# A gated block of long convolution and MLP on one core: first-layer weights in one transfer, the first layer in 256-token halves, full-shape filter matmuls, and early loads without a chain

## The chip, the cores and the metric

The kernel runs on one core of a Trainium2 chip. The metric is the device time of one execution in microseconds (us); lower is better. "The kernel before" and "the kernel after" are the two versions. The span of a profile, from the first to the last instruction, is about 2 us shorter than the device time.

In the profile PE is TensorE's matmuls, PEld its weight loads, DVE is VectorE, ACT is ScalarE, POOL is GpSimd and SP is SyncE, whose queue issues most DMA. A name with a q at the end (ACTq) is the engine's sequencer, which issues its instructions and DMA. PSUM is the memory that TensorE writes its results to; copying them out is called eviction. The "taps" are the weights of the 4-tap shift, brought into place by TensorE and ACT.

## The reference

```python
x = A_q                                            # 2048 tokens x 640, bf16
g = sigmoid((x * gate_w).sum(-1, keepdims=True))
# branch A: 4-tap shift of k, times v, a convolution over all 2048 tokens, times q
kv = shift(k, shift_k) * v
y  = irfft(rfft(pad(kv)) * rfft(pad(ssm_k)))[:2048] + kv * ssm_D
a  = q * y
# branch B: LayerNorm, first layer, token shifts by +1, -1, +2, -2 of the four quarters, second layer, MLP
h  = gelu(layernorm(x) @ w1)
x1 = x + shift_quarters(h) @ w2
b  = x1 + gelu(layernorm(x1) @ w3) @ w4            # 640 -> 1536 -> 640
out = g * a + (1 - g) * b
```

The kernel does the convolution as a folded discrete Fourier transform with matmuls. "Filter matmuls" transform the filter `ssm_k`, in five chunks of 128 features. "Chunks" of branch B are four groups of 512 tokens; a tile is 128 tokens. `mm1` to `mm4` are its four layers.

## The kernel before

The program is recorded as about 1200 operations with the memory that each reads and writes. A list scheduler then orders them for all engines at once; semaphore waits follow from the order. A table of about 350 numbers ("biases"), found by search, shifts the priorities. So the order of each engine's instructions is fixed at build time.

Large loads are chained: each waits for the landing of an earlier one.

```python
# in schedule()
if o.cost > 500 and not o.tp:                     # a large load that is not a transpose
    gate = [(ops[d].end, d) for d in done if ops[d].end <= st]
    if gate:
        o.preds.setdefault(max(gate)[1], False)   # wait for an earlier DMA
```

The first-layer weights come in eight transfers of small rows on ACT's queue, that is in the queue of the engine that also evicts PSUM:

```python
w1d = B_w1.rearrange("(c p) (g f) -> p c g f", p=128, g=4)
for g in range(4):
    P.dma("act", w1[:, g], w1d[:, :, g, 0:128])                              # rows of 256 B
for g in range(4):
    P.dma("act", w1[:, 4, :, 32 * g:32 * (g + 1)], w1d[:, :, g, 128:160])    # rows of 64 B
```

Each first-layer chunk is done at 512 tokens; its last feature tile is evicted in four 32-row pieces:

```python
def mm1(sc):
    xt = chunk_of[0, sc]
    ...                                            # gate products, 20 matmuls of one column
    for ft in range(5):
        pr = ps(1, "mm1")                          # one PSUM bank
        mm(pr, [(w1[:, ft, c], xt[:, c, :]) for c in range(DC)])
        if ft < 4:
            act(hT[:, ft, 2 + 512 * sc:2 + 512 * (sc + 1)], pr, ACTF.Gelu_apprx_tanh)
        else:
            for g in range(4):
                ...                                # 32 rows each, shifted
```

Two kinds of filter matmuls do not use the full 128 x 128 array:

```python
pairs = [(Rh[...], ev[...]) for kk in range(2)]
if y == 0:
    pairs.append((ones[0:1, :], ev[0:1, 1, :, 0, :]))              # 1 row
mm(pr[:, r, :], pairs, low=[(Zn[:, kk, :], ev[:, 0, :, kk, :])     # 32 columns
                            for kk in range(2)] if j == 0 and r == 1 else [])
```

Tokens of tiles 0 to 3 are transposed by TensorE and evicted by ACT; those of all later tiles by DMA. For `ln2`, ACT squares each tile for its sum alone, and the squared tile is discarded into `xn2[t % 2]`, the buffer from which a transposing DMA later reads:

```python
act(xn2[t % 2], X[:, t, :], ACTF.Square, scale=D ** -0.5, accum=st[1, 1][:, t:t + 1])
```

## Time and profile before

| | before |
|---|---|
| time, median of 4 runs | 261.24 us (260.86 to 263.06) |
| span of the profile | 259.0 us |
| first matmul of the first layer | 19.3 us |
| matmul time needed after the warm-up | 223.3 us |

The last row is my sum over all matmuls of the pitch (time from start to start) that undisturbed stretches of the trace show: 0.136 us for 320 columns, 0.216 us for 512 and 0.025 us for one, which columns / 2.4 ns plus 2.5 ns, and 0.025 us at least, fits.

The profile's page of the kernel before: the span, the busy line of all engines, and the busy tenths of each engine in 40 slices of 6.5 us (PEclk is the granted TensorE clock in tenths; DMA is the busy share of the 16 DMA engines).

```profile
span 259.0 us, 4011 instructions
...
PE 239.6 (93%) x1488; PEld 138.5 (53%) x1488; DVE 221.4 (85%) x337; ACT 166.6 (64%) x306; POOL 59.4 (23%) x93
...
PE   7189799999899999999999989999999999999970
...
DVE  4659378989798984438999899999999999999885
ACT  2172699879889985999934366323832275437993
...
PEclk9855999999999999999999999999999999999996
DMA  6999978996889999997124010000000000003776
...
```

PE is at 9 nearly everywhere except in the first 30 us and the last 8. This does not by itself prove a limit, because ends of matmuls are modelled. The start-to-start pitches do: after 30 us only 8.9 us of PE's time are not filled at full pitch. The page shows DVE at 9 from 150 to 240 us and DMA at mostly 7 to 9 for the first 120 us.

Three pieces of the chain that ended last (start us, length us, what). Buffer numbers are left out of names, so all four weights read `in_B_w_dram`; at this place it is the first layer's:

```profile
...
2.88 8.86 DMA arena<-in_B_w_dram
...
12.18 0.70 ACT arena L997
...
19.16 8.61 PE PSall L1008 x30
...
```

The same place in the timeline (start us, length us, engine, line, operation; in brackets the engine's idle time before it and what ended it):

```profile
...
3.92 8.22 ACTq L229 DMA_DIRECT2D arena<-in_B_w_dram  x4
...
12.18 0.69 ACT L997 ACTIVATE arena<-PSall 4x640 bf16<-4x640 bf16 x1 [8.37 <-DMA arena<-in_B_w_dram]
...
19.16 9.21 PE L1008 MATMUL PSall<-arena 128*128 128x1 bf16 x47 [0.30 <-ACT arena L997]
...
20.12 0.15 PEld L1008 LDWEIGHTS PSall<-arena 128*128 128x128 bf16 x1 [0.28 <-issue]
20.54 0.15 PEld L1008 LDWEIGHTS PSall<-arena 128*128 128x128 bf16 x1 [0.28 <-issue]
...
```

ACT's queue is held for 8.2 us by four of the weight transfers. The eviction at 12.18 us, which needs nothing but the taps, stands behind it. The first-layer matmuls begin within the group at 19.16 us (gate products first). The last two lines are weight loads of that group, 0.42 us apart, so a 512-column matmul takes 0.43 us instead of 0.216: half clock.

Weight loads by shape (count, total busy us, mean ns, then idle before and what ended it):

```profile
...
L1008 PEld LDWEIGHTS PSall<-arena 128*128 128x128 bf16 x1417 | 131.9, 98 | 98.0 <-ACT arena L997 9.5 <-issue 8.0 <-DVE arena L987 2.1
...
L1008 PEld LDWEIGHTS PSall<-arena 1*128 1x128 bf16 x10 | 0.9, 90 | 4.2 <-issue 4.2
L1008 PEld LDWEIGHTS PSall<-arena 128*32 128x32 bf16 x10 | 0.6, 94 | 1.1 <-issue 1.1
...
```

A load of 1 row or of 32 columns is no dearer than a full one (90 to 98 ns), but the ten 1-row loads have 4.2 us of idle time before them, put down to "issue". In the trace, a matmul on either side of a change of shape starts 0.31 us after the one before, not 0.216.

### The profile page before, as it was taken

The numbers are of one execution on the slowest core, as the hardware profiler recorded it, in microseconds if no ns is written. First come the engines' busy times: TensorE is split into PE (matmuls) and PEld (weight loads), VectorE is DVE, ScalarE is ACT, GpSimd is POOL, SyncE is SP. The second block draws the span as 40 slices with busy tenths as digits, with TensorE's granted clock in tenths as the row PEclk, the third lists the DMA queues.
The fourth block names the chain that finished last, engine by engine and source line by source line (L and its number), as shares of the span: only waits on it lengthen the run. The fifth ranks groups of instructions, "written<-read, shape, count | busy, mean of one in ns | idle before, by whom it ended". The sixth has DMA issues, their size and how long they took to land.

```text
span 259.0 us, 4011 instructions
## 1 busy us (share of the span) xinstructions
PE 239.6 (93%) x1488; PEld 138.5 (53%) x1488; DVE 221.4 (85%) x337; ACT 166.6 (64%) x306; POOL 59.4 (23%) x93
## 2 busy tenths in 40 slices
PE   7189799999899999999999989999999999999970
PEld 3063456744645464455466734566447754777750
DVE  4659378989798984438999899999999999999885
ACT  2172699879889985999934366323832275437993
POOL 2220054753970445113075500000000000000000
PEclk9855999999999999999999999999999999999996
DMA  6999978996889999997124010000000000003776
GB/s 174 273 257 179 324 253 137 195 239 179 171 187 237 225 257 240 281 288 221 36 51 124 16 25 9 16 3 0 0 3 0 0 4 0 0 3 110 210 187 202
DMA packets 66567, 34.42 MB, mean 133 GB/s; under 512 B 38008, under 2 KB 64884, under 8 KB 66548
## 3 DMA queue, kind: packets, MB, share of 16 engines
q1 hardware_dynamic: 59692, 32.71, 51.4%
q10 hardware_dynamic: 6712, 0.92, 2.7%
q0 software_dynamic: 144, 0.54, 0.7%
q8 instruction: 11, 0.18, 0.3%
q14 instruction: 8, 0.07, 0.1%
HBM read 24.34 MB, written 2.62 MB: 104 GB/s over the span
## 4 chain that ended last, share of the span: by engine, by line
PE 50%; DVE 21%; DMA 9%; ACT 9%; POOL 6%; issue 3%; ACTq 1%; POOLq 0%; SPq 0%
PE PSall L1008 50%; DVE arena L987 20%; ACT arena L997 9%; DMA arena<-arena 5%; POOL arena L992 4%; DMA arena<-in_B_w_dram 3%; POOL arena L1175 2%; DMA out_dram<-arena 1%; DVE arena L992 1%; ACTq L229 1%; DVE arena L1171 0%; POOLq L1402 0%; ACT L997 0%; DVE arena L1172 0%; SPq L226 0%
## 5 line engine op out<-in xcount | busy, mean ns | idle before, releaser
L1008 PE MATMUL PSall<-arena 128*128 128x320 bf16 (+4 forms) x1445 | 231.7, 319 | 10.3 <-ACT arena L997 9.1
L987 DVE TENSOR_TENSOR arena<-arena 128x640 bf16<-128x640 bf16 (+5 forms) x235 | 194.6, 877 | 9.7 <-ACT arena L997 7.5
L1008 PEld LDWEIGHTS PSall<-arena 128*128 128x128 bf16 (+2 forms) x1445 | 134.4, 98 | 107.5 <-issue 13.4
L997 ACT ACTIVATE arena<-PSall 128x640 bf16<-128x640 f32 (+5 forms) x186 | 118.1, 686 | 42.2 <-PE PSall L1008 33.0
L992 POOL TENSOR_SCALAR arena<-arena 128x1 f32<-128x1 f32 (+2 forms) x60 | 35.3, 592 | 85.7 <-ACT arena L997 64.7
L997 ACT ACTIVATE arena<-arena 128x640 bf16<-128x640 bf16 (+5 forms) x55 | 33.5, 619 | 21.1 <-DVE arena L987 11.5
L997 ACT ACTIVATE arena<-PSall,arena 128x640 bf16<-128x640 f32 (+1 forms) x32 | 20.4, 651 | 23.0 <-PE PSall L1008 22.9
L992 DVE TENSOR_SCALAR arena<-arena 128x640 bf16<-128x640 bf16 (+1 forms) x37 | 14.4, 402 | 18.1 <-POOL arena L1175 15.8
L1175 POOL TENSOR_TENSOR arena<-arena 128x1 f32<-128x1 f32 (+1 forms) x25 | 22.2, 889 | 1.4
L1171 DVE BATCH_NORM_STATS2 arena<-arena 128x6 f32<-128x320 bf16 x32 | 14.2, 477 | 4.8 <-DMA arena<-in_A_q_dram 4.8
L1034 PE MATMUL PSall<-arena 128*128 128x512 bf16 x18 | 5.6, 481 | 1.6 <-DVE arena L1030 1.6
L1034 PEld LDWEIGHTS PSall<-arena 128*128 128x128 bf16 x18 | 2.1, 120 | 4.6 <-issue 1.9
L997 ACT ACTIVATION_READ_ACCUMULATOR arena<-arena 128x1 f32 x16 | 3.4, 210 | 0.0
L997 ACT ACTIVATION_READ_ACCUMULATOR arena<-PSall 128x1 f32 x16 | 3.3, 204 | 0.0
L1172 DVE BATCH_NORM_AGGREGATE arena<-arena 128x2 f32<-128x12 f32 x16 | 2.8, 200 | 0.0
L997 ACT ACT_TABLE_LOAD x1 | 1.3, 1283 | 2.3 <-issue 2.3
L1226 PE MATMUL PSall<-arena 128*128 128x128 bf16 x20 | 2.5, 309 | 0.0
L1067 PE MATMUL PSall<-arena 128*4 128x128 bf16 x5 | 0.4, 218 | 2.1 <-DMA arena<-in_A_shift_k_dram 2.1
L1226 PEld LDWEIGHTS PSall<-arena 128*128 128x128 bf16 x20 | 2.0, 139 | 0.0
L992 DVE TENSOR_SCALAR arena<-PSall 128x4 f32<-128x4 f32 x4 | 0.6, 153 | 1.4 <-PE PSall L1008 1.4
L1067 PEld LDWEIGHTS PSall<-arena 128*4 128x4 bf16 x5 | 0.3, 83 | 2.6 <-DMA arena<-in_A_shift_k_dram 2.6
L987 POOL TENSOR_TENSOR arena<-arena 128x16 f32<-128x16 f32 x3 | 1.4, 476 | 0.5 <-DVE arena L992 0.4
(16 smaller groups left out, 3.4 us busy)
## 6 DMA issues: line engine op xcount, KB each, us to landing
arena<-in_A_k_dram SPq DMA_DIRECT2D x14, 400.0 KB, 4.5
arena<-in_A_q_dram SPq DMA_DIRECT2D x20, 160.0 KB, 2.5
arena<-in_A_v_dram SPq DMA_DIRECT2D x16, 160.0 KB, 4.7
arena<-in_A_ssm_k_dram SPq DMA_DIRECT2D x5, 512.0 KB, 4.5
out_dram<-arena SPq DMA_DIRECT2D x16, 160.0 KB, 2.3
arena<-in_A_q_dram SPq DMA_DIRECT2D x3, 640.0 KB, 5.7
arena<-in_B_w_dram SPq DMA_DIRECT2D x1, 1920.0 KB
arena<-in_B_w_dram SPq DMA_DIRECT2D x1, 1152.0 KB
```

Of the source, the lines that this page charges most:

```text
L229: fn = lambda e: e.dma_start(out, in_, **kw)
L987: P.op(eng, lambda e: e.tensor_tensor(o, a, b, op), [a, b], [o], dve_ns(o, [a, b], 2) if eng == "dve" else 500)
L992: P.op(eng, lambda e: e.tensor_scalar(o, real(a), s1, s2, op0=op0, **({} if op1 is None else {"op1": op1})), [a] + aps, [o], dve_ns(o, [a] ...
L997: P.op("act", lambda e: e.activation(o, real(a), f, bias=bias, scale=scale, **({"accum_out": accum} if accum is not None else {})), [a] + ...
L1008: fns.append(lambda e, part=part, l=l, r=r, i=i: e.matmul(real(o)[0:32] if part else real(o), l, r, start=(i == 0), stop=(i == last)))
L1034: P.op("pe", [lambda e: e.matmul(real(pw), warm[:, 0:128], warm[:, 128:640], start=True, stop=True)] * 2, [warm], [pw], 856.0)
L1067: P.op("pe", [lambda e, c=c: e.transpose(real(psb)[:, 128 * c:128 * (c + 1)], shk_sb[:, 4 * c:4 * c + 4], ident) for c in range(DC)], [shk ...
L1171: P.op("dve", lambda e, o=o, i=i: e.bn_stats(o, i), [i], [o], 400)
L1172: P.op("dve", lambda e: e.bn_aggr(bna[:, t, :], bns[k]), [bns[k]], [bna[:, t, :]], 120)
L1175: P.op("pool", lambda g: g.tensor_tensor(o, a, e, ALU.pow), [a, e], [o], 450 + 400 * n_of(o))
L1226: P.op("pe", [lambda e, c=c, pb=pb, xn=xn: e.transpose(real(pb)[:, 128 * c:128 * (c + 1)], xn[:, 128 * c:128 * (c + 1)], ident) for c in r ...
```

## The change

The intent is to get TensorE to real work sooner and to keep it there. It loads the first-layer weights with 1280 B rows in one transfer on SP, after four x tiles; splits the first layer of chunks 0 and 1 into halves of 256 tokens; transposes tiles 4 to 7 on TensorE too; pads the odd filter matmuls to 128 x 128 with zeros; and leaves early loads out of the chain. The bias table is new as a whole.

```diff
-                if o.cost > 500 and not o.tp:
+                if o.cost > 500 and not o.tp and not o.early:
...
-    w1d = B_w1.rearrange("(c p) (g f) -> p c g f", p=128, g=4)
-    for g in range(4):
-        P.dma("act", w1[:, g], w1d[:, :, g, 0:128])
-    for g in range(4):
-        P.dma("act", w1[:, 4, :, 32 * g:32 * (g + 1)], w1d[:, :, g, 128:160])
+    P.dma(sp, w1, B_w1.rearrange("(c p) f -> p c f", p=128), early=True)
+    act(w1x..., w1...[:, :, :, 128:160], ACTF.Copy)     # collects the last feature tile
...
-                    pairs.append((ones[0:1, :], ev[0:1, 1, :, 0, :]))
-                mm(..., low=[(Zn[:, kk, :], ev[:, 0, :, kk, :]) ...])
+                    pairs.append((Zn[:, 2, :], ev[:, 1, :, 0, :]))
+                if j == 0 and r == 1:
+                    pairs += [(Zn[:, kk, :], ev[:, 0, :, kk, :]) for kk in range(2)]
...
-            if t >= 4:
+            if t >= PET:                                # PET = 8: tiles 4 to 7 turned by TensorE
...
-        at(mm1, sc)
+        for k in (0, 1) if sc < 2 else (None,):         # halves in chunks 0 and 1
+            at(mm1, sc, *(() if k is None else (k,)))
+        at(mmg, sc)                                     # gate products apart
...
-    WARM = 9
+    WARM = 12                                           # 24 warm-up matmuls, not 18
-    BIASES = {...}
+    BIASES = {...}                                      # all values new
```

Cut: the loads of x for later chunks become two per chunk, the table of the filter transform moves from POOL's queue to SP's, the scheduler's engines begin at small offsets instead of 0, tiles 2 and 3 are normalised one by one, two costs in the scheduler's model change, an unused branch of `ln1` goes.

## The prediction

> **What bounds it now.** The page: span 259.0 us, TensorE (PE) busy 93%, DVE 85%, ACT 64%. The windows view shows three stages. From 0 to 30 us PE is badly fed: in the timeline the first-layer matmuls start at 19.2 us and chunk 0 of that layer ends at 28.4 us. From 30 to 251 us PE is back to back: the matmuls there, at their pitch in the trace (0.136 us for 320 columns, 0.216 us for 512), fill all but about 5 us. Then comes a tail of 7.5 us. VectorE is nearly as full (100% from 150 to 240 us), and DMA is near 100% until 120 us.
>
> **Why it starts late.** The chain of waits begins with 8.9 us of first-layer weight DMA: ACT's queue is stuck issuing small-row transfers (one group of issues spans 3.9 to 12.1 us), so the taps' eviction waits until 12.2 us. The same traffic delays the later x tiles (about 8 and 11.5 us) and the taps' input (6.7 us to landing). PE goes idle, and the layer's first 13 or so matmuls run at half clock, 0.43 us instead of 0.216 (clock row: 0.50 from 15 to 25 us), about 3 us lost. The Trainium skill, "TensorE: Matmul & The Clock Gate", section "What's actually happening", says that an idle window throttles the clock to half; this trace agrees.
>
> **What the change does.**
> 1. Weights in one transfer with 1280 B rows, behind four x tiles: ACT's queue is free; x tiles and taps land by 5 to 6 us. About 2.5 MB end with the weights; at the trace's 260 GB/s that is some 10 us plus 2 us to landing. I expect the layer's first matmul at 12 to 13 us, 6 to 7 us earlier, perhaps at full clock.
> 2. Halves, and PE transposes for tokens 4 to 7: PE keeps its columns plus 20 transposes (1.1 us); ACT gains some 6 us, and will pace PE between 12 and 30 us. By 30 us I expect chunks 0 and 1 and one second-layer tile done: 7 us ahead of before.
> 3. Full-shape filter matmuls: around each 1-row and 32-column group the pitch is 0.31 us instead of 0.216; six switches a chunk at 0.1 us, five chunks: 3 us, all on PE's chain.
> 4. Unchained early loads, and four DMA transposes fewer (1.3 us of SP queue each): they let DMA and VectorE keep up with the earlier PE; no separate gain.
> The re-tuned order gives nothing certain; 0 to 2 us may go to new PE waits on VectorE and DMA.
>
> **Prediction.** 7 + 3 us off 261.4: **251.0 us**, range 247.0 to 256.0. Faster by over 2%: 0.89; within 2%: 0.10; slower: 0.01.
>
> **What would show it.** First-layer matmuls from about 12.5 us; no 8 us issue on ACT's queue; x tiles landed by 6 us; pitch 0.216 us around filter matmuls; PE continuous from about 30 us, ending near 241 us; tail still 7 to 8 us; PE busy time 3 to 6 us lower.
>
> **What would make it wrong.** The filter and table loads (1 MB) ahead of the weights make them land after 15 us; the second-layer weights, k or v come late, standing behind 1.3 MB of x; VectorE, full in the last 100 us, does not move forward with PE, so PE waits for the products; or PE still starts at half clock.

## The result, and the profile after

| | before | after |
|---|---|---|
| median of 4 runs each | 261.24 us | 253.15 us |
| range | 260.86 to 263.06 | 252.32 to 253.76 |
| span of the profile | 259.0 us | 250.5 us |
| first matmul of the first layer | 19.3 us | 13.5 us |

The ratio is 0.9675, with a 95% interval of 0.9622 to 0.9728. The kernel is faster by 3.2%, and the time lies inside the predicted range.

The page after, the same rows as before:

```profile
span 250.5 us, 4194 instructions
...
PE 236.6 (94%) x1564; PEld 143.4 (57%) x1564; DVE 223.0 (89%) x337; ACT 171.9 (69%) x327; POOL 73.0 (29%) x94
...
PE   7999999999999999999997979999999999999990
...
DVE  5678889849999998898988899999999999998685
ACT  2699996999788999797724572236622286727993
...
PEclk9999999999999999999999999999999999999998
DMA  6999999987799996596522210000000000303676
...
```

The hole in PE's first 30 us is gone; the rest looks as before, and DVE now fills more of its row.

The pieces of the chain that ended last at the same place:

```profile
...
3.08 6.22 DMA arena<-in_A_ssm_k_dram
9.32 4.09 ACT arena L1012 x7
13.46 6.11 PE PSall L1021 x70
...
```

And the timeline at the same places:

```profile
...
4.12 0.43 SPq L230 DMA_DIRECT2D arena<-in_B_w_dram  x1
...
7.82 0.69 ACT L1012 ACTIVATE arena<-PSall 4x640 bf16<-4x640 bf16 x1 [3.94 <-PE PSall L1077]
...
13.46 6.11 PE L1021 MATMUL PSall<-arena 128*128 128x256 bf16 x70 [0.46 <-ACT arena L1012]
...
```

The weights are issued at 4.1 us in 0.4 us, ACT evicts the taps at 7.8 us, when TensorE has made them, and the first layer starts at 13.5 us instead of 19.3, at full pitch (0.109 us for 256 columns). It waits last for ACT's evictions of transposed tokens, no longer for weights.

The full-shape weight loads after, where the "issue" part of their idle time was 8.0 us and is 0.5 us (part of the 8.0 is the half clock at the start; the other two shapes are gone):

```profile
...
L1021 PEld LDWEIGHTS PSall<-arena 128*128 128x128 bf16 x1487 | 137.8, 98 | 92.4 <-ACT arena L1012 9.6 <-DVE arena L1002 2.8 <-issue 0.5
...
```

Waits, before and then after (waiter, what it waited for, us in total, times, longest):

```profile
...
PE PSall L1008 <- ACT arena L997: 9.1, 7, 3.2
...
ACT arena L997 <- DMA arena<-arena: 7.8, 3, 4.3
...
```

```profile
...
ACT arena L1012 <- DMA arena<-arena: 11.5, 8, 3.0
...
PE PSall L1021 <- ACT arena L1012: 4.6, 7, 1.6
...
```

PE waits less for ACT, but ACT now waits more often for transposing DMAs (`arena<-arena`): that is the new wait, and run 8 below is about it.

The ledger of PE, worked out from the starts of the matmuls in the two profiled traces (us; both hold as many matmuls as weight loads, so no record is missing). "Lost" is pitch beyond the undisturbed one.

| | before | after |
|---|---|---|
| useful matmul time issued by 30 us | 9.2 | 18.4 |
| useful matmul time in all | 223.3 | 224.6 |
| lost after 30 us at changes of shape | 3.0 | 0.0 |
| lost after 30 us in gaps of 0.25 us or more | 4.9 | 6.3 |
| lost after 30 us in smaller ones | 1.0 | 1.3 |
| from the last matmul's end to the span's end | 5.4 | 6.3 |

So 9.2 us of a head start, less 1.2 us of added matmuls; plus 3.0 us of shapes; less 1.7 us of new waits and 0.9 us of tail. That makes 8.3 of the span's 8.5 us (the rest is rounding and the last matmul's own length).

The head start is more than the earlier start of the layer, which is 5.8 us. Between that start and 30 us the kernel before loses about 2.9 us at half clock (14 matmuls, the first and last of them in part) and 1.8 us in a wait at 28.2 us for ACT, which evicts the last feature tile in four 32-row pieces; the kernel after loses 0.8 us. By the layer's start, the kernel after had done 0.5 us less of other matmuls. No run here takes away the half clock of the kernel before alone.

### The profile page after: what moved, and what is told of

The parts are those of the page before. It is cut to its first block, busy times and chain, and to the rows that moved or that the text cites. A ratio compares the mean times of both kernels' runs of the same rounds, so it can differ in the third digit from the quotient of the medians. Undisturbed runs are those within 1.5% of the kernel's fastest.

```text
span 250.5 us, 4194 instructions
## 1 busy us (share of the span) xinstructions
PE 236.6 (94%) x1564; PEld 143.4 (57%) x1564; DVE 223.0 (89%) x337; ACT 171.9 (69%) x327; POOL 73.0 (29%) x94
## 4 chain that ended last, share of the span: by engine, by line
PE 44%; DVE 17%; ACT 14%; DMA 11%; POOL 9%; issue 3%; SPq 1%; DVEq 0%; ACTq 0%; POOLq 0%
PE PSall L1021 43%; DVE arena L1002 15%; ACT arena L1012 14%; DMA arena<-arena 8%; POOL arena L1007 7%; DMA arena<-in_A_ssm_k_dram 2%; POOL arena L1187 2%; DVE arena L1007 1%; DMA arena<-in_A_q_dram 1%; SPq L230 1%; PE PSall L1228 1%; DVEq L443 0%; ACTq L443 0%; DVEq L441 0%; POOLq L441 0%
## 5 line engine op out<-in xcount | busy, mean ns | idle before, releaser
L1021 PE MATMUL PSall<-arena 128*128 128x320 bf16 (+4 forms) x1495 | 225.9, 311 | 5.9 <-ACT arena L1012 4.6
L1021 PEld LDWEIGHTS PSall<-arena 128*128 128x128 bf16 (+1 forms) x1495 | 138.4, 98 | 93.4 <-ACT arena L1012 9.6
L1012 ACT ACTIVATE arena<-PSall 128x640 bf16<-128x640 f32 (+8 forms) x206 | 121.5, 645 | 26.4 <-PE PSall L1021 21.6
L1007 POOL TENSOR_SCALAR arena<-arena 128x1 f32<-128x1 f32 (+2 forms) x61 | 46.2, 761 | 59.2 <-ACT arena L1012 39.7
L1012 ACT ACTIVATE arena<-arena 128x640 bf16<-128x640 bf16 (+4 forms) x55 | 34.5, 629 | 29.6 <-DVE arena L1002 15.8
L1012 ACT ACTIVATE arena<-PSall,arena 128x640 bf16<-128x640 f32 (+1 forms) x32 | 20.4, 660 | 16.8 <-PE PSall L1021 16.7
L1187 POOL TENSOR_TENSOR arena<-arena 128x1 f32<-128x1 f32 (+1 forms) x26 | 25.5, 984 | 1.6
L1183 DVE BATCH_NORM_STATS2 arena<-arena 128x6 f32<-128x320 bf16 x32 | 13.6, 476 | 3.9 <-DMA arena<-in_A_q_dram 3.9
L1047 PE MATMUL PSall<-arena 128*128 128x512 bf16 x24 | 7.9, 492 | 1.6 <-DVE arena L1043 1.6
L1047 PEld LDWEIGHTS PSall<-arena 128*128 128x128 bf16 x24 | 2.7, 121 | 5.7 <-issue 3.2
L1228 PEld LDWEIGHTS PSall<-arena 128*128 128x128 bf16 x40 | 2.3, 97 | 1.0 <-DVE arena L1183 0.4
L1141 DVE MEMSET arena<- 32x480 uint32 x2 | 0.9, 458 | 0.1
```

Source lines behind the costliest of these rows:

```text
L1007: P.op(eng, lambda e: e.tensor_scalar(o, real(a), s1, s2, op0=op0, **({} if op1 is None else {"op1": op1})), [a] + aps, [o], dve_ns(o, [a] ...
L1012: P.op("act", lambda e: e.activation(o, real(a), f, bias=bias, scale=scale, **({"accum_out": accum} if accum is not None else {})), [a] + ...
L1021: fns.append(lambda e, l=l, r=r, i=i: e.matmul(real(o), l, r, start=(i == 0), stop=(i == last)))
L1047: P.op("pe", [lambda e: e.matmul(real(pw), warm[:, 0:128], warm[:, 128:640], start=True, stop=True)] * 2, [warm], [pw], 856.0 if i < 4 els ...
L1141: P.op("dve", lambda e: e.memset(kt[0:32, 0:3, :], 0.0), [], [kt[0:32, 0:3, :]], 500)
L1183: P.op("dve", lambda e, o=o, i=i: e.bn_stats(o, i), [i], [o], 400)
```

## The experiments

My theory is the ledger: the early start and the shapes give the gain, because TensorE has no slack after 30 us. Rivals: the re-tuned table gives it; the clock gives it; VectorE sets the end, so that TensorE's savings come back as waits.

To undo one part alone, the order must not move. In the runs said to have "the same order" the scheduler was given the other build's order and PSUM places, operation by operation; waits are then worked out anew from the memory that is touched. Fed back to the unchanged kernel after, this reproduced it: a build of both programs differs in line numbers only. The helper's lines shift in these files, so line numbers differ from those above. All twelve kernels gave the correct result. Every call had its own runs of the kernel before; their medians were 261.51, 261.65 and 261.62 us.

| run | median us (range of 4) | ratio to before, 95% interval |
|---|---|---|
| 1 after, odd shapes put back | 255.48 (254.31 to 255.86) | 0.9763, 0.9721 to 0.9805 |
| 2 before, full shapes alone | 259.79 (258.75 to 260.47) | 0.9937, 0.9886 to 0.9988 |
| 3 after, small-row weights on ACT's queue | 263.77 (263.67 to 264.48) | 1.0094, 1.0057 to 1.0130 |
| 4 after, small-row weights on SP's queue | 257.13 (256.66 to 258.71) | 0.9845, 0.9799 to 0.9890 |
| 5 after, early loads chained | 253.75 (253.02 to 254.47) | 0.9707, 0.9678 to 0.9737 |
| 6 after, no real warm-up | 253.80 (253.17 to 254.13) | 0.9706, 0.9680 to 0.9732 |
| 7 after, whole 512-token chunks | 261.66 (261.31 to 263.50) | 1.0024, 0.9984 to 1.0065 |
| 8 after, squares into a free buffer | 251.45 (251.04 to 252.45) | 0.9624, 0.9588 to 0.9660 |
| 9 before, empty table | 287.23 (285.00 to 287.32) | 1.0945, 1.0893 to 1.0997 |
| 10 after, empty table | 307.99 (307.29 to 308.54) | 1.1757, 1.1716 to 1.1798 |
| 11 after, whole chunks, their own order | 266.65 (264.95 to 268.09) | 1.0178, 1.0111 to 1.0244 |
| 12 after, tiles 4 to 7 turned by DMA | 257.79 (256.88 to 258.01) | 0.9845, 0.9808 to 0.9881 |

### 1. The odd filter shapes put back into the kernel after

```diff
-                    pairs.append((Zn[:, 2, :], ev[:, 1, :, 0, :]))
-                if j == 0 and r == 1:
-                    pairs += [(Zn[:, kk, :], ev[:, 0, :, kk, :]) for kk in range(2)]
+                    pairs.append((ones[0:1, :], ev[0:1, 1, :, 0, :]))
+                mm(..., low=[(Zn[:, kk, 0:32], ev[:, 0, :, kk, :]) ... if j == 0 and r == 1 else []])
```

> The kernel after, in the same order on every engine, with the ten 1-row and ten 32-column filter matmuls put back in place of the full-shape ones. My theory (a change of shape costs TensorE about 0.1 us each time, six times a chunk, and TensorE has no slack there): 253.2 plus 2.5 to 3.2, so 255.7 to 256.4 us. Rival (the switches hide behind waits for VectorE and DMA, which set the pace): within 1 us of 253.2.

Measured: 255.48 us, 2.3 us more than 253.15 (the two ranges of four do not overlap, though the intervals of the ratios just touch). Weight loads by shape in this run:

```profile
...
L1186 PEld LDWEIGHTS PSall<-arena 1*128 1x128 bf16 x10 | 0.9, 90 | 4.2 <-issue 4.2
...
L1186 PEld LDWEIGHTS PSall<-arena 128*32 128x32 bf16 x10 | 0.6, 94 | 1.1 <-issue 1.1
...
```

The idle time before the two shapes is back to the figure of before, 4.2 and 1.1 us, and the ledger has 3.0 us lost at 30 changes of shape (12 of the 1564 matmul records are missing from this trace). My theory holds, a little below its stated range; the rival, under 1 us, does not.

### 2. Full shapes alone in the kernel before

The edit is that of the change, with the table of zeros widened from 64 to 384 columns.

> The kernel before, in its own order, with full-shape filter matmuls alone. My theory: 261.2 minus 2.5 to 3.2, so 258.0 to 258.7 us. Rival: VectorE, full from 150 us on in the trace of before, sets the end, so TensorE's 3 us come back as waits and the time stays within 1 us of 261.2.

Measured: 259.79 us, 1.7 us less, with an interval of the ratio from 0.9886 to 0.9988. So it helps, but with a little over half of the 3.0 us that PE's ledger loses at these places. In this run's ledger nothing is lost at changes of shape; 13 of the 1488 matmul records are missing from its trace, and allowing for those (2.6 us), the losses after 30 us are 7.1 us where before had 8.9. The 1.8 us between them answer to the time; about 1.2 of the 3.0 us came back as waits, 0.5 us of it in the last gap before the end (2.6 us at 249 us, for 2.1 at 251). Both accounts have a share. The layer began 1.1 us later in this run (20.4 us), yet by 30 us TensorE had done as much as in the kernel before (allowing for one missing record), so a small shift at the start need not reach the end.

### 3 and 4. The weights in eight small-row transfers again

```diff
-    P.dma(sp, w1, w1s, early=True)
+    w1op = P.dma("act", w1, w1s, early=True)            # run 3; sp in run 4
+    w1op.fns = [lambda e, a=a, b=b: e.dma_start(w1[:, :, a:b], w1s[:, :, a:b])
+                for a, b in [(160*g + 128, 160*g + 160) for g in range(4)]
+                          + [(160*g, 160*g + 128) for g in range(4)]]
```

> The kernel after, in the same order, with the first-layer weights again in eight small-row transfers (256 B and 64 B rows) on ACT's queue. My theory (the weight load is what delayed the start): the first layer starts 3 to 6 us later than 13.5 us, ACT's queue is stuck for some us, and the time rises to 256 to 259 us. Rival (the start is set by the tokens, taps and transposes, and the weights have slack): at most 1 us slower.

> The same eight small-row transfers, but issued by SP in the place of the one transfer, so that ACT's queue stays free. If the row size and the traffic are what costs: nearly as slow as with ACT's queue, 255 to 258 us. If the stuck ACT queue is what costs: within 1.5 us of 253.2.

Measured: 263.77 us on ACT's queue, 10.6 us more than the kernel after and 2.3 us more than before; 257.13 us on SP's, 4.0 us more. ACT's timeline in run 3:

```profile
...
4.10 13.06 ACTq L1233 DMA_DIRECT2D arena<-in_B_w_dram  x6
17.21 0.69 ACT L1177 ACTIVATE arena<-PSall 4x640 bf16<-4x640 bf16 x1 [13.30 <-issue]
...
```

ACT's sequencer sits on six issues for 13.1 us, and everything that ACT should evict waits. The first layer starts at 23.5 us, 10.0 us later than in the kernel after, and the time grows by nearly the same 10.6 us: here a later start passes straight through to the end. (The layer's first 12 matmuls run at half clock in this run, 1.2 us of pitch.) TensorE's timeline in run 4:

```profile
...
11.26 1.54 PE L1396 MATMUL PSall<-arena 128*128 128x128 bf16 x20
15.53 4.78 PE L1186 MATMUL PSall<-arena 128*128 128x256 bf16 x27 [2.73 <-DMA arena<-in_B_w_dram]
```

Here ACT is free and TensorE waits 2.7 us for the weights themselves; the layer starts at 15.5 us, and the x loads and second-layer weights behind it come later too: the eight issues hold SP's queue for 8.3 us, and the next x load is issued at 12.5 us instead of 4.6. So about 4 us belong to eight small-row transfers instead of one, the held SP queue included, and another 6.6 us to having them in ACT's queue. Row size and number of transfers were changed together. Nor is row size all: in the kernel after, two of SP's issues of long rows (x and second-layer weights) took 2.0 and 1.8 us, where others took 0.4. What stretches an issue is not shown. My forecast for run 3 (256 to 259) was too low by 5 us, since I had not thought that the same order would put all six issues ahead of ACT's first eviction.

The Trainium skill ("DMA: Bandwidth & Descriptors", section "Issuing engines are not separate DMA queues") says that issuing from several engines saves only the sequencer's time to start a DMA, "which is usually small relative to the DMA itself". In this trace it is not small: 13.1 us of one sequencer for six of the eight transfers, when all the weights in one transfer took 0.43 us to issue in the kernel after.

### 5. The early loads chained again

```diff
-EARLY = lambda o: o.early
+EARLY = lambda o: False       # for the waits only; the order is the same
```

> The kernel after, in the same order, with the early loads chained again: each large load waits for the landing of an earlier one, as in before. My theory: the chain holds back the loads behind the first tokens by some us, so the first layer starts 1 to 4 us later and the time rises by 1 to 4 us, to 254 to 257. Rival (the queue is full anyway, and order alone matters): within 0.7 us of 253.2.

Measured: 253.75 us, 0.6 us more, which the intervals do not separate from nothing. The first layer starts at 13.6 us instead of 13.5. In this order the chain hardly bites; the rival is right. The run says nothing of the chain in the kernel before, where two of its waits stand in ACT's queue.

### 6. No real warm-up

```diff
-e.matmul(real(pw), warm[:, 0:128], warm[:, 128:640], start=True, stop=True)
+e.matmul(real(pw)[:, 0:32], warm[:, 0:128], warm[:, 128:160], start=True, stop=True)
```

> The kernel after, in the same order, with the 24 warm-up matmuls cut from 512 to 32 columns, so that TensorE does nearly nothing before its first real work. If the clock state at the first layer matters: the granted clock is 0.5 for the first 3 to 6 us of the first layer, and the time rises by 1.5 to 3 us, to 254.7 to 256.2. If ACT's evictions pace the first layer (I predicted so): within 1 us of 253.2.

Measured: 253.80 us, 0.65 us more and not separated from nothing. The profile shows the layer beginning at 12.9 us with 9 matmuls of 256 columns at a pitch of 0.213 us, twice the usual 0.109: half clock, but for only 2 us. The start itself is no later than with the warm-up (12.9 to 13.6 us in runs 1, 5 and 8). Half clock costs 1.1 us of pitch here, and 0.65 us or less of it reaches the time. The number meets my second expectation, but not for its reason: the stretch was short, and ACT did not pace the layer. The run prices the warm-up of the kernel after. It does not price the half clock of the kernel before (2.9 us in the ledger), so the clock as a rival is only in part refuted. This is the place to warn of the clock column (a stretch of the windows view: busy us of each engine with its count, then the granted clock, DMA share and GB/s):

```profile
...
core 0: us, PE busy (x) PEld busy (x) DVE busy (x) ACT busy (x) POOL busy (x), PEclk, DMA share, GB/s
13.00:16.00 3.00, 3.00 (x19) 2.24 (x19) 2.80 (x9) 2.59 (x6) 0.71 (x2) 1.00 1.07 362
...
```

The column says 1.00 from 13 to 16 us, where the pitch says half. The Trainium skill ("TensorE: Matmul & The Clock Gate", section "Seeing it yourself") warns that these clock events have been "observed to be unreliable"; this trace agrees. (In the kernel before, the column did show 0.50 from 15 to 25 us, where the pitch is half.) The pitch between matmuls is the better witness.

### 7 and 11. Whole chunks in the place of halves

```diff
-        for k in (0, 1) if sc < 2 else (None,):
+        for k in (None,):
```

> The kernel after, in the same order, with the first layer of chunks 0 and 1 in whole 512-token matmuls in the place of the second half. The first layer must wait for four transposed tokens, not two: about 1.4 us later in the trace of after (13.5 to 14.9 us), while ACT saves about 3 us of evictions. My theory: 253.2 plus 0.5 to 2 us. Rival (ACT paces this stage): 253.2 or less.

Measured: 261.66 us, 8.5 us more: all of the gain. TensorE's timeline from 14 to 40 us:

```profile
...
15.27 7.47 PE L1184 MATMUL PSall<-arena 128*128 128x512 bf16 x45 [1.66 <-ACT arena L1175]
22.60 0.72 PE L1391 MATMUL PSall<-arena 128*128 128x128 bf16 x10
24.74 1.80 PE L1184 MATMUL PSall<-arena 128*128 128x320 bf16 x12 [1.42 <-ACT arena L1175]
26.39 0.72 PE L1391 MATMUL PSall<-arena 128*128 128x128 bf16 x10
28.22 7.20 PE L1184 MATMUL PSall<-arena 128*128 128x512 bf16 x37 [1.11 <-ACT arena L1175]
37.56 2.88 PE L1184 MATMUL PSall<-arena 128*128 128x320 bf16 x14 [2.14 <-ACT arena L1175]
```

The layer starts at 15.3 us (1.8 us later, and the 6 first matmuls are at half clock), and then TensorE waits for ACT before each group: 1.4, 1.1 and 2.1 us. With halves, ACT evicts the first half while TensorE does the second, and the first second-layer tile needs only the first half. With whole chunks, in this order, the two engines take turns; in the kernel before, TensorE's wait for ACT at 28.2 us is of the same kind. I had expected 0.5 to 2 us. The order was made for halves, though, so in run 11 the scheduler ordered whole chunks itself:

> The kernel after with whole 512-token matmuls in chunks 0 and 1, as in the run that took 261.7 us, but here the scheduler makes its own order for them (the table kept, its entries for the halves gone). If the 8.5 us of that run came from an order made for halves: 254 to 256.5 us here. If halves are needed to keep ACT and TensorE overlapped at the start whatever the order: 258 us or more.

Measured: 266.65 us, slower still. This meets the number that I had named for "halves are needed whatever the order" (258 or more), but run 11 lacks tuned entries for its new operations, and runs 9 and 10 show what a missing entry can cost. Two orders out of very many don't prove that no order would do.

### 8. The discarded squares into a free buffer

ACT's line in the kernel after, in the stretch of the longest gaps of TensorE:

```profile
...
129.08 0.74 ACT L1012 ACTIVATE arena<-arena 128x640 bf16<-128x640 bf16 x1 [3.02 <-DMA arena<-arena]
...
132.68 0.74 ACT L1012 ACTIVATE arena<-arena 128x640 bf16<-128x640 bf16 x1 [2.77 <-DMA arena<-arena]
...
133.41 1.46 ACT L1012 ACTIVATE arena<-PSall,arena 128x640 bf16<-128x640 f32 x2
...
```

ACT waits 3.0 and 2.8 us for transposing DMAs that still read the buffer into which the square is discarded; since ACT works in order, the PSUM eviction at 133.41 us, for which TensorE waits, stands behind it.

```diff
-        act(xn2[t % 2], X[:, t, :], ACTF.Square, ...)
+        act(xn2[t % 2] if t < 8 else xn1[2], X[:, t, :], ACTF.Square, ...)   # and placed behind its eviction
```

> The kernel after, with one fix: for tiles 8 to 15 the discarded output of ACT's squares goes to a free buffer instead of the one that the transposes still read, and the squares stand right behind their evictions. My theory: ACT's 11.5 us of waits for transposes, and TensorE's two gaps of 1.8 and 1.6 us at 132 and 144 us that come from ACT standing still, mostly go; 253.2 minus 1.5 to 3 us. Rival: VectorE is full from 150 us, so the gaps only move: within 0.7 us of 253.2.

Measured: 251.45 us, 1.7 us less by medians. The same stretch in this run:

```profile
...
132.09 0.79 ACT L1175 ACTIVATE arena<-PSall,arena 128x640 bf16<-128x640 f32 x1 [7.49 <-PE PSall L1184]
133.86 0.79 ACT L1175 ACTIVATE arena<-PSall,arena 128x640 bf16<-128x640 f32 x1 [0.97 <-PE PSall L1184]
...
```

ACT's waits for transposes are gone, and with them TensorE's gaps at 132 and 144 us (1.8 and 1.6 us). But four squares now stand between ACT's evictions from 102 to 107 us, where the kernel after has two, and a new gap opens there, at 106 us:

```profile
...
PE PSall L1184 <- ACT arena L1175: 1.5, 1, 1.5
```

Gaps of 0.25 us or more after 30 us sum to 5.85 us, where the kernel after has 6.34. So the gaps mostly moved, as the rival said, though the time did improve: this is the fastest kernel of the study. Its interval (0.9588 to 0.9660) overlaps that of the kernel after (0.9622 to 0.9728), so the step over the kernel after is likely but not settled. The run changes two things, the buffer and the place of the squares in ACT's order; which of them counts was not tested.

### 9 and 10. Both kernels with an empty table

```diff
-    P.biases.update(BIASES)
+    P.biases.update({})
```

> The kernel before with its table of order biases emptied: its scheduler orders by its own rule alone. Theory (the change of structure gives most of the 8 us): both kernels lose by the same kind of amount and the kernel after with an empty table stays 5 us or more ahead of this one. Rival (the re-tuned table gives the gain): both without a table end within 3 us of each other.

> The kernel after with its table of order biases emptied. Theory: 5 us or more faster than the kernel before with an empty table. Rival: within 3 us of it. Either way slower than 253, by how much I can't say: 258 to 275.

Measured: before 287.23 us, after 307.99 us. Both of my statements fail: without its table the kernel after is not 5 us ahead, nor is it within 3 us, but 21 us behind, and its time is far outside the 258 to 275 that I named. Its longest wait of TensorE for ACT is 29 us:

```profile
...
PE PSall L1021 <- ACT arena L1012: 41.5, 15, 29.0
...
```

The table is worth 26 us to the kernel before and 55 us to the kernel after, several times the whole change. So the change cannot be split cleanly into structure and order: the gain is that of a structure and an order fitted to it. The runs at a fixed order show what each part does inside that order, and nothing more.

### 12. Tiles 4 to 7 turned by DMA again

```diff
-    PET = 8
+    PET = 4
```

> The kernel after, in the same order, with tokens of tiles 4 to 7 transposed by DMA again (1.2 us of SP queue each, some 3 us to landing) in the place of TensorE and ACT. My prediction gave this part no gain of its own. If that is right: within 1 us of 253.2. If the SP queue and the landing hold back chunk 1: 255 to 259 us, with TensorE waiting for a DMA near 22 us.

Measured: 257.79 us, 4.6 us more. TensorE:

```profile
...
24.42 4.54 PE L1184 MATMUL PSall<-arena 128*128 128x256 bf16 x25 [2.68 <-DMA arena<-arena]
29.94 6.32 PE L1184 MATMUL PSall<-arena 128*128 128x256 bf16 x50 [0.97 <-DMA arena<-arena]
```

It waits 2.7 and 1.0 us for transposing DMAs before the two halves of chunk 1. I had given this part no gain of its own; inside this order it carries 4.6 us.

## Why the prediction was right, and where it was not

The time (253.15 us for 251.0, in a range of 247 to 256) and the sign were right.

- **The head start was right.** "6 to 7 us earlier" for the first layer: 19.3 to 13.5 us, 5.8 us. "7 us ahead of before" by 30 us: 9.2 us of useful matmuls more, 8.0 after taking off the added ones. Run 3 shows that a shift of the start by 10.0 us shifts the end by 10.6 us. The size owes something to luck: the start itself moved less than forecast, and the rest of the 9.2 us came from half clock and a wait for ACT, for which the sum has no term. "ACT's queue is stuck issuing" holds for 6.0 of its 8.2 us; 2.2 us were waits of the chain, which the prediction counted for nothing.
- **The shapes were right in mechanism and too large in time.** "3 us, all on PE's chain": PE's ledger loses exactly 3.0 us there, and none after. But undone in the kernel after it costs 2.3 us and alone in the kernel before it gives 1.7 us: not all of it was on the chain.
- **The size that was missing** is the sentence "0 to 2 us may go to new PE waits". I named it and took nothing off. The ledger has 1.7 us more of waits after 30 us and 0.9 us more of tail. TensorE's last matmul ended at 244 us, not near 241. That is more than the distance to 251; the head start, 1 us larger than forecast, made up for some, so part of the closeness is errors that cancel.
- **"ACT … will pace PE between 12 and 30 us" did not happen.** TensorE lost 0.8 us from the layer's start at 13.5 us to 30 us. Run 7 shows why the halves matter there: in that order they are what keeps ACT from pacing it.
- **"Perhaps at full clock" was right; its worth is open.** In before, half clock costs the layer 2.9 us of pitch, part of the head start above. Run 6 shows only that without its warm-up the kernel after has 1.1 us of half clock and loses 0.65 us, within the noise.
- **"No separate gain" for the unchained loads and the transposes was half right.** Chaining again costs 0.6 us, within the noise; the transposes by DMA cost 4.6 us.
- **"The re-tuned order gives nothing certain" was the weakest sentence.** Order is worth more than everything else here (runs 9 and 10). Undoing single parts inside the tuned order costs 10.6, 8.5, 4.6, 2.3, 0.6 and 0.6 us, in sum over three times the gain; a likely reason, not shown, is that the order was fitted to all of them. What a table newly searched for the old structure would reach is open; no run here can say.

## What to carry to other kernels

Where TensorE is back to back to the end, look at when it starts: a much later start can pass through to the end nearly in full (run 3), and the cause may be a compute engine whose own queue is stuck issuing small-row DMA. Put such issues on a queue that evicts nothing, in as few transfers as possible, and cut the first work so that the evicting engine can begin while TensorE goes on. In a statically ordered kernel, undo a part with the order held before saying what it is worth, and do not add such costs up.

## What the Trainium skill lacked or had wrong

- "TensorE: Matmul & The Clock Gate" (section "Step-by-step: what each phase is for") says that weight loads are pulled ahead of running matmuls where row groups don't conflict or the load goes to the background buffer. Neither it nor "TensorEngine Tiling (Array Packing)", which has a change of tiling mode drain TensorE, gives a price for a change of array shape: here each change to or from a 1-row or 32-column matmul costs about 0.1 us (pitch 0.31 instead of 0.216 us for 512 columns), although the loads themselves take 90 to 98 ns in any shape. Whether these changes are such a drain is not shown.
- "DMA: Bandwidth & Descriptors" calls the sequencer's time to start a DMA usually small. "Perfetto Trace Analysis" does describe a sequencer as taken up until a DMA's descriptors are made. What both lack is how long that can be for an engine with other work: six transfers of 256 B and 64 B rows held ACT for 13.1 us (run 3).
- "TensorE: Matmul & The Clock Gate" is right that clock events are unreliable. For a cross-check it names a throttle counter; the pitch serves too: 0.213 us for 256 columns showed half clock where the recorded clock was 1.00 (run 6).
